# Row broadcasts by DMA instead of matmuls, and weight-sum stores issued by SyncE, in a tuned transformer block

## Chip, cores, metric

One core of a Trainium2 chip. The metric is the device time of one launch in microseconds (us): the median of several runs, and for comparisons the ratio to runs of the kernel before on the same chip. TensorE is called PE in the profile, VectorE DVE, ScalarE ACT, GpSimd POOL, SyncE SP.

## The reference, cut to what matters

```python
mod = silu(c) @ w_mod                      # six rows of 1024: sa, ca, ga, sb, cb, gb
h = layernorm(x) * (1 + ca) + sa
x = x + ga * attention(h)                  # 2048 queries, 32 heads of 128, 512 keys
h = layernorm(x) * (1 + cb) + sb
x = x + gb * (silu(h @ w_gate) * (h @ w_up)) @ w_down
```

`ga` and `gb` (the gate rows) multiply along the free dimension, so each has to stand in all 128 partitions. So has `silu(c)` (the conditioning row), because VectorE computes the late columns of `mod` as row products with transposed `w_mod` tiles. The large products are done with seven instead of eight block products, for which sums of weight blocks are made on VectorE during attention, stored to DRAM, and read back later.

## The kernel before

A row that sits as a column (one value per partition, eight columns) was spread by matmul: a ones matrix times a diagonal holding the column.

```python
def row_task(dst, dbuf, src, sbuf):
    ACT: c6 <- src                                           # 128x8
    def diags(n):
        for q in range(4):
            ACT: diag[q] <- ident * c6[:, 4*n+q]             # 128x128
    diags(0); yield
    for n in range(2):
        for q in range(4):
            mm(bank(XB, P, q * P), ones_bf, diag[q], q == 0, q == 3, ...)
        DVE: dst[:, n*512:(n+1)*512] <- bank(XB)
        if n == 0: diags(1)
        yield
```

The units of weight sums run in two slots of SBUF (the core's on-chip memory). Each unit is a load, four subtractions and a store; the fourth sum overwrites a quarter of the raw weights, so a slot's next load waits for its store to land:

```python
Q_of = {o: (dq("q_sl%d" % o, nc.gpsimd), dq("q_sw%d" % o, nc.gpsimd)) for o in OFF_ST}
# load of unit k into slot k % 2
T.op(Q_of[slot][0], lambda: g.dma_start(dst, src), reads=ahead, writes=[w.b_raw, w.b_s3])
# ... four DVE subtractions, spread over the iterations of attention ...
T.op(Q_of[slot][1], lambda: g.dma_start(dst, w.four), reads=[w.b_s3] + w.b_s, writes=[B_uw[units[k]]])
```

The softmax here doesn't subtract the row's maximum and nothing guards it: scores larger than these inputs give would overflow.

Of the kernel before, what the change touches and what calls it, by code (L numbers as in the profile page):

```python
# [4 lines left out]
AF = mybir.ActivationFunctionType  # L5
BF16 = mybir.dt.bfloat16
F16 = mybir.dt.float16
F32 = mybir.dt.float32
P = 128
# [122 lines left out]
def bass_adaLN_cond__sliding_block_cached__swiglu_ffn__prompt_kernel(  # L132
# [51 lines left out]
    mhalf = S_("mhalf", [P, TPC], F32)  # L184
    c_row = S_("c_row", [DT, P], BF16)
    sc_bf = S_("sc_bf", [P, DT], BF16)
    mod_bf = S_("mod_bf", [P, NJ], BF16)
    c6 = S_("c6", [P, DT], F32)
    mcol = S_("mcol", [P, 4 * DT], F32)
    gain = [S_("gain%d" % i, [P, DT], BF16) for i in range(2)]  # L190
    gain_f = S_("gain_f", [P, DT], F32)
# [20 lines left out]


    OFF_H20 = 154 * KB
    B_ident = _Buf("ident"); B_ones = _Buf("ones"); B_zw = _Buf("zw")
    B_diag = [_Buf("diag%d" % i) for i in range(4)]
    ident = arena.at(OFF_H20, [P], BF16, [B_ident])
    ones_bf = arena.at(OFF_H20 + 256, [P], BF16, [B_ones])
    diag = [arena.at(OFF_H20 + 512 + 256 * i, [P], BF16, [B_diag[i]]) for i in range(4)]
    zwarm = arena.at(OFF_H20 + 2048, [512], BF16, [B_zw])  # L220

    def bank(b, n=512, off=0):
# [5 lines left out]
    def bank_bf(b):  # L228
        return ps[:, b * 512:(b + 1) * 512].bitcast(BF16)
# [4 lines left out]
    PB = [_Buf("bank%d" % b) for b in range(8)]  # L234
    B_x = [_Buf("x%d" % t) for t in range(ST)]
    B_mh = _Buf("mhalf")
    B_cT = _Buf("cT"); B_sc = _Buf("sc"); B_late = [_Buf("late%d" % i) for i in range(4)]; B_c6 = _Buf("c6"); B_mcol = _Buf("mcol"); B_scr = _Buf("scr")
    B_mode = _Buf("mode"); B_modc = _Buf("modc"); B_bq = _Buf("bq"); B_gf = _Buf("gf")
    B_nm = _Buf("nmean"); B_acc = _Buf("acc"); B_acc0 = _Buf("acc0")
    B_g = [_Buf("g%d" % i) for i in range(2)]  # L240
# [21 lines left out]
    with nc.Block() as block:  # L262

        @block.gpsimd
        def _(g):
# [23 lines left out]
            def finish(gen):  # L289
                while gen in bg:  # L290
# [4 lines left out]
            T.op(POOL, lambda: g.affine_select(out=ident, in_=ident, compare_op=ALU.not_equal,  # L295
                                               fill=1.0, base=0, pattern=[[-1, P]], channel_multiplier=1),
                 reads=[B_ident], writes=[B_ident])
            T.op(POOL, lambda: g.memset(ones_bf, 1.0), writes=[B_ones])
            T.op(POOL, lambda: g.memset(mhalf[:, :], -0.5), writes=[B_mh])
            T.op(POOL, lambda: g.memset(zwarm, 0.0), writes=[B_zw])  # L300

# [115 lines left out]
            for gk in range(1, Hkv):  # L417
                load_kT(gk)
                load_v(gk)
            T.op(POOL, lambda: g.memset(v_aug[:, :, P:P + 2], 1.0), writes=[B_va])  # L420


            B_ns4 = B_ns + [_Buf("ns2"), _Buf("ns3")]
# [103 lines left out]
            def mod_ca(hf, k):  # L527
# [5 lines left out]
            T.op(PE, lambda: TE.transpose(bank_bf(XB)[:, 0:DT], c_row[:, :], ident[0:DT, 0:DT]),  # L533
                 reads=[B_cT, B_ident], writes=[PB[XB]])
            T.op(ACT, lambda: A.activation(sc_bf[:, :], bank_bf(XB)[:, 0:DT], AF.Silu), writes=[PB[XB], B_sc])
            T.op(ACT, lambda: A.activation(acc[:, 0:1], mhalf[:, 0:1], AF.Exp), reads=[B_mh], writes=[B_acc])


# [71 lines left out]
                     reads=[B_mcol], writes=[cbuf])  # L610


            def row_task(dst, dbuf, src, sbuf):
                T.op(ACT, lambda: A.activation(c6[:, :], src, AF.Copy), reads=[sbuf], writes=[B_c6])

                def diags(n):
                    for q in range(4):
                        col = 4 * n + q
                        T.op(ACT, lambda: A.activation(diag[q], ident, AF.Copy, scale=c6[:, col:col + 1]),
                             reads=[B_ident, B_c6], writes=[B_diag[q]])  # L620

                diags(0)
                yield
                for n in range(2):
                    for q in range(4):
                        mm(bank(XB, P, q * P), ones_bf, diag[q], q == 0, q == 3, [B_ones, B_diag[q]], PB[XB], skip=True)
                    T.op(DVE, lambda: V.tensor_copy(dst[:, n * 512:(n + 1) * 512], bank(XB)),  # L627
                         writes=[PB[XB], dbuf])
                    if n == 0:
                        diags(1)  # L630
                    yield


            LEAD = 3
# [290 lines left out]
                    mm(bank(bk), la, ra, start and k == 0, k == HK - 1, [lb, rb], PB[bk], skip=True)  # L925


            Q_of = {o: (dq("q_sl%d" % o, nc.gpsimd), dq("q_sw%d" % o, nc.gpsimd)) for o in OFF_ST}
            units = [("o", p) for p in range(HP)] + [("d", p) for p in range(FP)]
            unit_of = {}  # L930
            B_uw = {u: _Buf("uw%s%d" % u) for u in units}
# [15 lines left out]
            def unit_sums(k):  # L947
                w, slot = unit_of.pop(k)
                r = w.raw.rearrange("p k n -> p (k n)")
                rf = w.rawf.rearrange("p k n -> p (k n)")  # L950
                b11, b12, b21, b22 = [r[:, 512 * n:512 * n + 512] for n in range(4)]
                e = [x.rearrange("p k n -> p (k n)") for x in w.s]
                R = w.b_raw
                for (o, a, b, rd, wr) in ((e[0], b12, b11, [R, w.b_s3], w.b_s[0]), (e[1], b22, e[0], [R, w.b_s[0]], w.b_s[1]),
                                          (e[2], b21, e[1], [R, w.b_s[1]], w.b_s[2]), (rf[:, 1536:2048], b22, b12, [R], w.b_s3)):
                    T.op(DVE, lambda: V.tensor_tensor(o, a, b, SUB), reads=rd, writes=[wr])  # L956
                    yield
                kind, p = units[k]
                dst = (wo_sum if kind == "o" else wd_sum)[p].rearrange("q a n -> q (a n)")
                T.op(Q_of[slot][1], lambda: g.dma_start(dst, w.four), reads=[w.b_s3] + w.b_s, writes=[B_uw[units[k]]])  # L960

            def unit_chain(k0, k1):
                after = _Buf("after")
# [218 lines left out]


            rows = None
            bgx = []

            def run_x():
                if bgx:
                    try:
                        next(bgx[0])  # L1190
                    except StopIteration:
                        bgx.pop(0)

            LOADX = {14: 2, 20: 3}
            TAKES = [12, 17, 61] + [i for i in range(15, 2 * NI - 15) if i % 4 == 3 or (i > NI + 2 and i % 4 == 2 and i % 5 in (1, 4))]
            TAKES = sorted(TAKES)[:NL]
            TAKET = {i: n for n, i in enumerate(TAKES)}
            LOADT = {max(i - 4, TAKES[max(n - 2, 0)] if n > 1 else 0): n for i, n in TAKET.items()}
            assert len(TAKES) == NL and len(LOADT) == NL and not {NI, NI + 1} & (set(TAKET) | set(LOADT))
            take_oT(0)  # L1200
# [23 lines left out]
            def mods(i):  # L1224
                if i in TAKET:
                    n = TAKET[i]
                    mod_col(n)
                    g0, last = divmod(n, DT)
                    if last == DT - 1:
                        mod_take(g0, B_late[g0])  # L1230
                        if g0 == 0:
                            bgx.append(row_task(rowb[0], B_row[0], mod_bf[:, 2 * DT:3 * DT], B_late[0]))
                        elif g0 == 2:
                            mod_gain(1, B_late[2], B_g[1])
                        elif g0 == 3:
                            bgx.append(row_task(rowb[1], B_row[1], mod_bf[:, 5 * DT:6 * DT], B_late[3]))
                if i in LOADT:
                    load_mt(LOADT[i])

            def both(a, b):  # L1240
                yield from a
# [6 lines left out]
            def pre0(i):  # L1248
                if 2 <= i < NQ0:
                    q_shifted(i)  # L1250
                if i in LOADX:
                    load_x(LOADX[i])
                if i == 1:
                    scores(0)
                if i in (1, 3):
                    q_bias_mm(i + 1, i + 3, XB)
                if i == 1:
                    for dt in range(HK, DT):
                        shift(dt)
                if i < 9:  # L1260
                    if 2 <= i < 7:
                        qproj(i + 4)
                    elif i == 7:
                        qproj_mm(ND - 1, QB, 0, HK)
                    elif i == 8:
                        qproj(ND - 1, k0=HK)
                        for dt in range(DT):
                            modulate(hT[1], B_hT[1], dt, 0, 0, B_mode, x1_tiles)
                elif i + 4 < NDI:
                    qproj(i + 3)  # L1270
                elif i + 4 == NDI:
                    qproj_mm(NDI - 1, QB, 0, HK)
                elif i + 3 == NDI:
                    qproj(NDI - 1, k0=HK)
                for n, tt in enumerate(NORMS.get(i, ())):
                    norm_turn(1, tt, x1_tiles, (i + n) % 2)
                if 2 <= i < 6:
                    next(x1_stats[1])
                if i == 8:
                    bgx.append(row_task(sc_row, B_scr, sc_bf[:, :], B_sc))  # L1280
                if i == ND + 2:
                    take_oT(2)
                    take_oT(3)
                mods(i)
                if i == 44:
                    bg.append(stats_task(2 * TPC, 2 * TPC))
# [5 lines left out]
            def tick0(i):  # L1292
                if 2 <= i < 6:
                    next(x1_stats[0])
                if i < 20 or i % 4 == 0:
                    run_x()
                if i == 21:
                    hs[0] = h_sums()
                if 21 <= i < 25:
# [133 lines left out]
                mods(i)  # L1433

            def tick1(i):
                if i % 4 == 0:
                    run_x()
                if i > NI:
                    wq_tick(1, i)
                    if i == NI + 1:  # L1440
                        chain[0] = unit_chain(HP, HP + FP)
                    if i < 2 * NI - 8:
                        unit_tick(i)

            take_wq(1, 2)
            attend(1, NI, pre1, tick1)
            while bgx:
                run_x()


            OFF_GU = [14 * KB * i for i in range(4)]
# [288 lines left out]
```

## Time and profile before

| | before |
|---|---|
| time, median of 3 | 1155.57 us (1154.97 to 1157.11) |
| profiled span | 1152.5 us |
| PE busy, without work | 1140.7 us, 11.8 us |
| stores of weight sums, issue to landing, median of the first 16 | 4.8 us |

The page gives busy time by engine; "the chain" follows the last instruction back to what released it, step by step, so its shares tell which engine sets the end. The wait views give total, number and longest wait; what is behind the arrow ended the wait. The prediction below shows the lines that bound this kernel. The time of stores is this row of the list of DMA issues (size, then median us from issue to landing):

```profile
wo_sum<-arena POOLq DMA_DIRECT2D x16, 512.0 KB, 4.8
```

### The profile page before, as it was taken

Reading aid. Unit: us, or ns where it says so; the run is one execution under the profiler, and the core shown is the slowest. Engines: PE = TensorE matmul, PEld = TensorE weight load, DVE = VectorE, ACT = ScalarE, POOL = GpSimd, SP = SyncE. Lnnn points to the kernel's source line nnn. Section 1 sums busy time; section 2 is a strip of 40 time slices with the busy share of each in tenths; the row PEclk is TensorE's granted clock in tenths of the full one; section 3 lists DMA queues with packets and bytes.
Section 4 is the critical chain, followed back from the end, with each engine's and each line's share of the span. In section 5 each row is a group of like instructions: output and inputs, shape, how many; then the busy total and the mean of one; then the engine's idle time right before and its main releaser. Section 6 shows DMA issues by size and latency. Waiting matters only on the chain.

```text
span 1152.5 us, 17997 instructions
## 1 busy us (share of the span) xinstructions
PE 1140.7 (99%) x6930; PEld 585.6 (51%) x7015; DVE 826.0 (72%) x1650; ACT 532.3 (46%) x745; POOL 66.5 (6%) x137
## 2 busy tenths in 40 slices
PE   8999999999999999999999999999999999999999
PEld 5566565554446665566444444444444444444444
DVE  5768779847667777776657789877658777776536
ACT  4857787720127777787110354444110444444110
POOL 1100112100000111111000000000000000000000
DMA  9879999986718999945774422323773433234443
GB/s 316 143 182 225 206 219 221 216 206 182 220 36 183 202 211 207 197 97 120 192 224 136 110 74 79 105 74 101 210 218 129 119 84 100 74 103 133 129 157 110
DMA packets 299572, 179.96 MB, mean 156 GB/s; under 512 B 140512, under 2 KB 288736, under 8 KB 299488
## 3 DMA queue, kind: packets, MB, share of 16 engines
q1 hardware_dynamic: 236512, 92.31, 37.6%
q10 hardware_dynamic: 54336, 55.05, 15.1%
q0 software_dynamic: 8640, 31.46, 8.8%
q8 instruction: 55, 0.90, 0.3%
q14 instruction: 29, 0.24, 0.1%
HBM read 125.96 MB, written 19.92 MB: 127 GB/s over the span
## 4 chain that ended last, share of the span: by engine, by line
PE 96%; DVE 1%; DMA 1%; issue 1%; ACT 0%; POOL 0%; POOLq 0%; DVEq 0%
PE ps L272 96%; DMA wo_sum<-arena 1%; DMA arena<-in_A_wo_dram 0%; ACT arena L805 0%; DVE arena L835 0%; DVE arena L956 0%; DVE arena L827 0%; PE ps L276 0%; DVE arena L906 0%; DVE arena L852 0%; DVE arena L604 0%; DVE rl L824 0%; DVE rowb L627 0%; POOL arena L300 0%; DVE tmp L1117 0%
## 5 line engine op out<-in xcount | busy, mean ns | idle before, releaser
L272 PE MATMUL ps<-arena 128*128 128x512 f16 (+2 forms) x6717 | 1135.6, 330 | 8.9 <-POOL arena L420 2.2
L272 PEld LDWEIGHTS ps<-arena 128*128 128x128 bf16 (+1 forms) x6802 | 578.5, 98 | 560.0 <-DVE arena L835 4.9
L805 ACT ACTIVATE arena<-ps 128x1024 bf16<-128x1024 f32 x256 | 261.5, 1021 | 44.4 <-PE ps L272 32.6
L838 ACT ACTIVATE tmp<-ps 128x512 f32<-128x512 f32 x167 | 99.7, 597 | 295.9 <-PE ps L272 289.9
L906 DVE TENSOR_TENSOR arena<-arena 128x512 f16<-128x512 bf16 x328 | 133.4, 419 | 3.0
L835 DVE TENSOR_TENSOR arena<-ps,tmp 128x512 bf16<-128x512 f32 (+1 forms) x134 | 91.9, 686 | 51.4 <-PE ps L272 34.7
L838 ACT ACTIVATE nsc<-ps 128x512 f32<-128x512 f32 x84 | 50.1, 597 | 93.3 <-PE ps L272 90.9
L827 DVE TENSOR_TENSOR arena<-ps,rl 128x512 f16<-128x512 f32 x128 | 88.5, 691 | 4.9 <-DVE rl L824 0.5
L835 DVE TENSOR_TENSOR arena<-ps,nsc 128x512 f16<-128x512 f32 x84 | 57.3, 687 | 40.3 <-PE ps L272 29.9
L824 DVE RECIPROCAL rl<-ps 128x4 f32<-128x4 f32 x128 | 23.3, 182 | 73.7 <-PE ps L272 72.5
L1555 ACT ACTIVATE arena<-arena 128x512 f16<-128x512 f16 x84 | 49.8, 624 | 32.8 <-DVE arena L835 32.8
L1046 DVE TENSOR_TENSOR arena<-arena 128x2048 f16<-128x2048 f16 (+3 forms) x56 | 56.0, 1011 | 9.3 <-PE ps L272 8.8
L1122 DVE TENSOR_TENSOR tmp<-ps,tmp 128x512 f32<-128x512 f32 x32 | 22.1, 690 | 55.5 <-ACT tmp L838 45.8
L838 ACT ACTIVATE arena<-ps 128x512 f32<-128x512 f32 x16 | 9.6, 597 | 87.8 <-PE ps L272 87.8
L956 DVE TENSOR_TENSOR arena<-arena 128x512 f16<-128x512 bf16 x120 | 47.9, 420 | 2.5 <-DMA arena<-in_A_wo_dram 1.5
L427 DVE BATCH_NORM_STATS2 st<-x_res 128x6 f32<-128x512 bf16 x58 | 39.6, 682 | 3.7 <-DMA x_res<-in_A_x_dram 3.4
L604 DVE SCALAR_TENSOR_TENSOR arena<-arena 128x1024 bf16<-128x1024 bf16 x32 | 38.9, 1216 | 0.0
L1570 DVE TENSOR_TENSOR arena<-arena 128x512 f16<-128x512 f16 x84 | 35.0, 417 | 0.3
L1123 DVE TENSOR_TENSOR tmp<-tmp,rowb 128x512 f32<-128x512 f32 (+1 forms) x49 | 33.6, 686 | 1.7
L441 DVE TENSOR_SCALAR nsc<-x_res,mv,rstd 128x1024 f16<-128x1024 bf16 (+1 forms) x30 | 16.2, 539 | 24.1 <-DMA arena<-nsc 24.0
L1124 DVE TENSOR_TENSOR arena<-tmp,x_res 128x512 bf16<-128x512 f32 (+1 forms) x33 | 22.3, 676 | 1.1
L835 DVE TENSOR_TENSOR arena<-ps,rowb 128x512 f16<-128x512 f32 x28 | 19.3, 689 | 3.8 <-ACT rowb L838 3.3
(86 smaller groups left out, 323.6 us busy)
## 6 DMA issues: line engine op xcount, KB each, us to landing
arena<-in_A_wq_dram SPq DMA_DIRECT2D x30, 512.0 KB, 5.3
arena<-wo_sum ACTq DMA_DIRECT2D x7, 2048.0 KB, 8.2
arena<-in_B_w_gate_dram SPq DMA_DIRECT2D x28, 512.0 KB, 4.0
arena<-in_B_w_up_dram SPq DMA_DIRECT2D x28, 512.0 KB, 5.1
arena<-wd_sum ACTq DMA_DIRECT2D x8, 1792.0 KB, 7.9
arena<-in_B_w_down_dram ACTq DMA_DIRECT2D x6, 1792.0 KB, 7.8
arena<-in_A_wo_dram POOLq DMA_DIRECT2D x16, 512.0 KB, 5.1
wo_sum<-arena POOLq DMA_DIRECT2D x16, 512.0 KB, 4.8
```

The lines of the kernel that those rows point to most:

```text
L272: T.op(PE, lambda: TE.matmul(out_ap, lhsT, rhs, start=start, stop=stop, skip_group_check=skip), reads=reads, writes=[bank_buf])
L427: T.op(DVE, lambda: V.bn_stats(st_[sl][:, hf * 6:hf * 6 + 6], x_res[:, t, hf * 512:hf * 512 + 512]), reads=[B_x[t]], writes=[B_st[sl]])
L604: T.op(DVE, lambda: V.scalar_tensor_tensor(mt[n % 2], mt[n % 2], 1.0, sc_row, op0=ALU.mult, op1=ALU.mult, accum_out=mcol[:, n:n + 1]), rea ...
L805: T.op(ACT, lambda: A.activation(ex_s[es][:, 2 * kp:2 * kp + 2, :], banks2(SCB + 2 * kp), AF.Exp, scale=att_scale), writes=[PB[SCB + 2 * k ...
L827: T.op(DVE, lambda: V.tensor_tensor(o_s[os_].rearrange("p (a b) d -> p a b d", a=2), psap(PVB * 512, [[512, 2], [130, 2], [1, P]]), rlb, A ...
L835: T.op(DVE, lambda: V.tensor_tensor(out, bank(ba), other, ADD), reads=[ob2], writes=[PB[ba], ob])
L838: T.op(ACT, lambda: A.activation(dst, bank(bk), AF.Copy), writes=[PB[bk], db])
L906: T.op(st, lambda: eng.tensor_tensor(o, a, b, op), reads=rd, writes=[wr])
L956: T.op(DVE, lambda: V.tensor_tensor(o, a, b, SUB), reads=rd, writes=[wr])
L1046: T.op(DVE, lambda: V.tensor_tensor(o, a, b, SUB), reads=rd, writes=[sb])
L1555: T.op(ACT, lambda: A.activation(o, s_, AF.Silu), reads=[sb], writes=[ob])
L1570: T.op(DVE, lambda: V.tensor_tensor(gu[blk][:, p, :], o, s_, MULT), reads=[sb, ob], writes=[B_gu[blk][p]])
```

## The change

Its intent: take the row matmuls off TensorE, their diagonals off ScalarE and their copies off VectorE, and let SyncE instead of GpSimd issue the stores of weight sums. A row now goes: columns transposed by DMA inside SBUF, stored to DRAM as eight runs of 256 bytes, read back with a zero stride over partitions. The conditioning row starts as a row, so it skips the transpose and gets a second Silu on ScalarE.

```diff
+T.op(POOL, lambda: g.memset(mod_bf[:, :], 0.0), ...)        # mod_bf is now 128x128; ones_bf, diag, c6 are gone
+T.op(ACT, lambda: A.activation(c_row[:, :], c_row[:, :], AF.Silu), writes=[B_cT])
-def row_task(dst, dbuf, src, sbuf): ...                     # as above
+def row_hop(n, hop):
+    if hop == 0:
+        T.op(Q_row[n][0], lambda: SP.dma_start_transpose(turned..., mod_bf[:, :]), reads=[B_mode] + B_late, writes=[B_turn])
+    elif hop == 1:
+        src, sb = (c_row[:, :], B_cT) if n == 2 else (turned[c0:c0 + DT, :], B_turn)
+        T.op(Q_row[n][1], lambda: SP.dma_start(rows_d[n], src), reads=[sb], writes=[B_rd[n]])
+    else:
+        every = bass.AP(tensor=rows_d[n].tensor, offset=0, ap=[[0, P], [1, D]])
+        T.op(Q_row[n][2], lambda: SP.dma_start(dst, every), reads=[B_rd[n]], writes=[db])
+HOPS = {4: (2, 1), 8: (2, 2)}                               # attention iteration: (row, hop)
+for n, i in ((0, TAKES[DT - 1]), (1, TAKES[NL - 1])):
+    HOPS.update({i + 2: (n, 0), i + 5: (n, 1), i + 8: (n, 2)})
-Q_of = {o: (dq("q_sl%d" % o, nc.gpsimd), dq("q_sw%d" % o, nc.gpsimd)) for o in OFF_ST}
+Q_of = {o: (dq("q_sl%d" % o, nc.gpsimd), dq("q_sw%d" % o)) for o in OFF_ST}
-T.op(Q_of[slot][1], lambda: g.dma_start(dst, w.four), ...)
+T.op(Q_of[slot][1], lambda: SP.dma_start(dst, w.four), ...)
```

More of the change, by code (lines that the diff above doesn't have):

```diff
@@ L186, in bass_adaLN_cond__sliding_block_cached__swiglu_ffn__prompt_kernel @@
     sc_bf = S_("sc_bf", [P, DT], BF16)
-    mod_bf = S_("mod_bf", [P, NJ], BF16)
-    c6 = S_("c6", [P, DT], F32)
+    mod_bf = S_("mod_bf", [P, P], BF16)
     mcol = S_("mcol", [P, 4 * DT], F32)
@@ L214, in bass_adaLN_cond__sliding_block_cached__swiglu_ffn__prompt_kernel @@
     OFF_H20 = 154 * KB
-    B_ident = _Buf("ident"); B_ones = _Buf("ones"); B_zw = _Buf("zw")
-    B_diag = [_Buf("diag%d" % i) for i in range(4)]
+    B_ident = _Buf("ident"); B_turn = _Buf("turn"); B_zw = _Buf("zw")
     ident = arena.at(OFF_H20, [P], BF16, [B_ident])
-    ones_bf = arena.at(OFF_H20 + 256, [P], BF16, [B_ones])
-    diag = [arena.at(OFF_H20 + 512 + 256 * i, [P], BF16, [B_diag[i]]) for i in range(4)]
+    turned = arena.at(OFF_H20 + 256, [P], BF16, [B_turn])
     zwarm = arena.at(OFF_H20 + 2048, [512], BF16, [B_zw])
@@ L236, in bass_adaLN_cond__sliding_block_cached__swiglu_ffn__prompt_kernel @@
     B_mh = _Buf("mhalf")
-    B_cT = _Buf("cT"); B_sc = _Buf("sc"); B_late = [_Buf("late%d" % i) for i in range(4)]; B_c6 = _Buf("c6"); B_mcol = _Buf("mcol"); B_scr = _Buf("scr")
+    B_cT = _Buf("cT"); B_sc = _Buf("sc"); B_late = [_Buf("late%d" % i) for i in range(4)]; B_mcol = _Buf("mcol"); B_scr = _Buf("scr")
     B_mode = _Buf("mode"); B_modc = _Buf("modc"); B_bq = _Buf("bq"); B_gf = _Buf("gf")
@@ L297, in _ @@
                  reads=[B_ident], writes=[B_ident])
-            T.op(POOL, lambda: g.memset(ones_bf, 1.0), writes=[B_ones])
             T.op(POOL, lambda: g.memset(mhalf[:, :], -0.5), writes=[B_mh])
@@ L420, in _ @@
             T.op(POOL, lambda: g.memset(v_aug[:, :, P:P + 2], 1.0), writes=[B_va])
+            T.op(POOL, lambda: g.memset(mod_bf[:, :], 0.0), writes=[B_mode] + B_late)
             B_ns4 = B_ns + [_Buf("ns2"), _Buf("ns3")]
@@ L610, in mod_take @@
                      reads=[B_mcol], writes=[cbuf])
-            def row_task(dst, dbuf, src, sbuf):
-                T.op(ACT, lambda: A.activation(c6[:, :], src, AF.Copy), reads=[sbuf], writes=[B_c6])
-                def diags(n):
-                    for q in range(4):
-                        col = 4 * n + q
-                        T.op(ACT, lambda: A.activation(diag[q], ident, AF.Copy, scale=c6[:, col:col + 1]),
-                             reads=[B_ident, B_c6], writes=[B_diag[q]])
-                diags(0)
-                yield
-                for n in range(2):
-                    for q in range(4):
-                        mm(bank(XB, P, q * P), ones_bf, diag[q], q == 0, q == 3, [B_ones, B_diag[q]], PB[XB], skip=True)
-                    T.op(DVE, lambda: V.tensor_copy(dst[:, n * 512:(n + 1) * 512], bank(XB)),
-                         writes=[PB[XB], dbuf])
-                    if n == 0:
-                        diags(1)
-                    yield
+            rows_d = [nc.dram_tensor("row%d" % n, [DT, P], BF16).ap() for n in range(3)]
+            B_rd = [_Buf("rowd%d" % n) for n in range(3)]
+            Q_row = [[dq("q_row%d_%d" % (n, m)) for m in range(3)] for n in range(3)]
+            def row_hop(n, hop):
+                if hop == 0:
+                    T.op(Q_row[n][0], lambda: SP.dma_start_transpose(turned.rearrange("p (a b) -> p a b", a=1), mod_bf[:, :]),
+                         reads=[B_mode] + B_late, writes=[B_turn])
+                elif hop == 1:
+                    c0 = (2 + 3 * n) * DT
+                    src, sb = (c_row[:, :], B_cT) if n == 2 else (turned[c0:c0 + DT, :], B_turn)
+                    T.op(Q_row[n][1], lambda: SP.dma_start(rows_d[n], src), reads=[sb], writes=[B_rd[n]])
+                else:
+                    dst, db = ((rowb[0][:, :], B_row[0]), (rowb[1][:, :], B_row[1]), (sc_row, B_scr))[n]
+                    every = bass.AP(tensor=rows_d[n].tensor, offset=0, ap=[[0, P], [1, D]])
+                    T.op(Q_row[n][2], lambda: SP.dma_start(dst, every), reads=[B_rd[n]], writes=[db])
             LEAD = 3
@@ L959, in unit_sums @@
                 dst = (wo_sum if kind == "o" else wd_sum)[p].rearrange("q a n -> q (a n)")
-                T.op(Q_of[slot][1], lambda: g.dma_start(dst, w.four), reads=[w.b_s3] + w.b_s, writes=[B_uw[units[k]]])
+                T.op(Q_of[slot][1], lambda: SP.dma_start(dst, w.four), reads=[w.b_s3] + w.b_s, writes=[B_uw[units[k]]])
             def unit_chain(k0, k1):
@@ L1184, in _ @@
             rows = None
-            bgx = []
-            def run_x():
-                if bgx:
-                    try:
-                        next(bgx[0])
-                    except StopIteration:
-                        bgx.pop(0)
             LOADX = {14: 2, 20: 3}
@@ L1230, in mods @@
                         mod_take(g0, B_late[g0])
-                        if g0 == 0:
-                            bgx.append(row_task(rowb[0], B_row[0], mod_bf[:, 2 * DT:3 * DT], B_late[0]))
-                        elif g0 == 2:
+                        if g0 == 2:
                             mod_gain(1, B_late[2], B_g[1])
-                        elif g0 == 3:
-                            bgx.append(row_task(rowb[1], B_row[1], mod_bf[:, 5 * DT:6 * DT], B_late[3]))
                 if i in LOADT:
                     load_mt(LOADT[i])
+                if i in HOPS:
+                    row_hop(*HOPS[i])
             def both(a, b):
@@ L1278, in pre0 @@
                     next(x1_stats[1])
-                if i == 8:
-                    bgx.append(row_task(sc_row, B_scr, sc_bf[:, :], B_sc))
                 if i == ND + 2:
@@ L1294, in tick0 @@
                     next(x1_stats[0])
-                if i < 20 or i % 4 == 0:
-                    run_x()
                 if i == 21:
@@ L1435, in tick1 @@
             def tick1(i):
-                if i % 4 == 0:
-                    run_x()
                 if i > NI:
@@ L1446, in _ @@
             attend(1, NI, pre1, tick1)
-            while bgx:
-                run_x()
             OFF_GU = [14 * KB * i for i in range(4)]
```

## The prediction

> **What bounds the kernel now.** I read the page's first part, then the chain that ended last, then the waits of TensorE, and last the rows of the instructions that the change touches.
>
> ```profile
> PE 1140.7 (99%) x6930; PEld 585.6 (51%) x7015; DVE 826.0 (72%) x1650; ACT 532.3 (46%) x745; POOL 66.5 (6%) x137
> PE 96%; DVE 1%; DMA 1%; issue 1%; ACT 0%; POOL 0%; POOLq 0%; DVEq 0%
> ```
>
> TensorE (PE) is busy for 1140.7 of 1152.5 us and holds 96% of the chain. A busy PE need not be a PE at its peak, so I compared starts of successive matmuls in the trace: 216 ns between 512-column ones, 57 ns between 129-column ones, nearly everywhere. Of the 11.8 us without work about 2.2 us come before the first matmul and 2.5 us at the end. So PE is held by its own list of matmuls, and a change pays in two ways only: by taking matmuls off the list, or by ending a wait of PE. Those waits between 20 and 1140 us, in full:
>
> ```profile
> PE ps L272 <- DVE arena L827: 0.7, 1, 0.7
> PE ps L272 <- DVE arena L835: 0.4, 2, 0.2
> PE ps L272 <- ACT arena L805: 0.3, 1, 0.3
> ```
>
> They sum to 1.4 us, the ceiling of the second way as far as this view sees it. The 0.7 us one is the only one with a DMA behind it. The timeline around it:
>
> ```profile
> 127.90 0.57 POOL L960 DMA_DIRECT2D wo_sum<-arena  x1 [2.08 <-DVE arena L956]
> ...
> 136.33 0.70 POOL L945 DMA_DIRECT2D arena<-in_A_wo_dram  x1 [7.86 <-DMA wo_sum<-arena]
> ...
> 141.53 0.88 DVE L956 TENSOR_TENSOR arena<-arena 128x512 f16<-128x512 bf16 x2 [1.48 <-DMA arena<-in_A_wo_dram]
> 142.33 1.22 DVE L604 SCALAR_TENSOR_TENSOR arena<-arena 128x1024 bf16<-128x1024 bf16 x1
> ...
> 144.83 2.40 PE L272 MATMUL ps<-arena 128*128 128x129 bf16 x21 [0.68 <-DVE arena L827]
> ```
>
> Read it downwards: the weight sums leave by a GpSimd DMA, the load into the same slot waits for that store to land (7.86 us), VectorE waits 1.48 us for the load, runs late with the softmax division (L827), and PE stands still for 0.68 us. It is the one place where a store of weight sums reaches PE.
>
> **What the Trainium skill says.** "TensorE: Matmul & The Clock Gate", section "Wait — 56ns, not 53.3ns?", gives 55.6 and 215.7 ns between starts of warm matmuls of 128 and 512 columns; this trace has 56 and 216 ns, so it agrees, and 56 ns is the price of each removed matmul. "DMA: Bandwidth & Descriptors", section "Issuing engines are not separate DMA queues", says that DMAs of all issuers run on the same 16 engines and that another issuer saves the sequencer's time alone: no bandwidth is to be had from moving the stores to SyncE. Section "SWDGE vs HWDGE vs iDMA" of that page calls the hardware path's set-up faster; its "Specifications" put the first byte at about 1 us for GpSimd and 0.6 us for SyncE, so I estimate 0.4 us per store. No run here shows that difference yet. The page's "Two DMAs through the same engine are not ordered" asks for a wait on the first DMA before one that reads what it wrote; the changed kernel has these waits, and they stand in SyncE's list, so I ask below whether they hold up others.
>
> **Removed: matmuls.** Three rows (conditioning row, gate rows 0 and 1) were spread over partitions by a ones matrix times diagonals: 3 rows x 2 halves x 4 = 24 matmuls of 128 columns. The instruction order of both builds shows that nothing else moves on PE: six groups of four are gone. Price: 24 x 56 ns = 1.34 us. The chain confirms that they cost their full length today. In the second attention stretch two kinds of iteration alternate, and those with four more matmuls are longer:
>
> ```profile
> 493.24 6.08 PE ps L272 x51
> 499.32 0.05 issue
> 499.37 6.94 PE ps L272 x55
> 506.31 0.05 issue
> 506.36 6.30 PE ps L272 x55
> 512.66 0.05 issue
> 512.72 6.94 PE ps L272 x55
> 519.66 0.05 issue
> 519.71 6.30 PE ps L272 x55
> ```
>
> 6.30 against 6.08 us is 0.22 us for four, that is 55 ns each; 6 x 0.22 = 1.32 us, the same sum.
>
> **Removed: work of ScalarE and VectorE.**
>
> ```profile
> L619 ACT ACTIVATE arena<-arena,c 128x128 bf16<-128x128 bf16 x24 | 7.6, 389 | 0.1
> L627 DVE CAST rowb<-ps 128x512 bf16<-128x512 f32 x4 | 2.7, 680 | 0.0
> L627 DVE CAST arena<-ps 128x512 bf16<-128x512 f32 x2 | 1.4, 680 | 0.0
> ```
>
> ScalarE loses 7.6 us of diagonals and three 0.2 us copies of columns, VectorE six casts or 4.1 us. None is on the chain except one cast, at 173.35 us, ahead of a 0.2 us wait of PE (the one on L835 near 176 us). Elsewhere the engines have room: VectorE is busy 29.4 of the 40 us from 60 to 100 and about 75% of 340 to 540. So from these 12 us I count 0.2 us.
>
> **Added.** ScalarE gets one Silu of 8x128 near 3.5 us; like its neighbour it should take some 0.18 us, and ScalarE then idles 1.97 us for x at 7.02. GpSimd swaps a ones memset for a zero memset of the same size (0.2 us) that stands after the one PE waits for; PE's first matmul can come about 0.2 us sooner, but the first projection at 11.67 us needs weights that landed at 11.48 us (the issue-to-landing times of that load), so I count zero. SyncE gets two 128x128 transposes, three 2 KB stores, three broadcasts of 256 KB. Estimated from like ones, 1.2 us of issue and some 4 us to landing for a transpose, 0.5 us of issue and 3 to 5 us to landing for a load. All have time: the conditioning row is asked for in iteration 8 (about 51 us) and first read at 64.8 us; gate row 0 arrives around iteration 43 (about 171 us) and is first read at 262.9 us; gate row 1 comes in iteration 119, read from about 886 us on. The bytes are 0.8 MB beside 180 MB.
>
> **Moved.** Thirty stores of 512 KB go from GpSimd to SyncE.
>
> ```profile
> L960 POOL DMA_DIRECT2D wo_sum<-arena x16 | 9.4, 591 | 66.8 <-DVE arena L956 66.8
> L960 POOL DMA_DIRECT2D wd_sum<-arena x14 | 8.0, 571 | 90.9 <-DVE arena L956 90.9
> ```
>
> GpSimd's 17 us of issue are worth nothing, it is 6% busy. SyncE has room: per iteration of about 3.4 us it issues one 1.2 us transpose, a weight-row transpose of 1.3 us in one of two to four, a query load of 0.53 us in one of four, and now a store of about 0.57 us in one of three: some 1.2 + 0.4 + 0.13 + 0.2 = 1.9 us. What matters is when the slot comes free. From issue to landing the 16 stores of the first attention took 3.5 to 9.1 us (the 14 of the second 3.1 to 5.8), and the next load 4 to 6 us more; the time left between that load's landing and its first use was 0.02 to 3.5 us for most of those from 100 to 215 us, and 4 us or more in the second attention, bar the first. At 127.14 us SyncE issued a weight-row transpose, landing at 135.83 us beside the slow store. The store now stands ahead of it in SyncE's list (it belongs to the iteration before), so I expect it to leave first and land in 4 to 5 us. Then VectorE's 1.48 us wait and PE's 0.68 us go. That gain I count in full: 0.7 us.
>
> **Sum.** 1.34 (matmuls) + 0.7 (the wait at 144 us) + 0.2 (the wait at 176 us) = 2.2 us, so 1155.57 - 2.2 = 1153.4 us.
>
> **Rivals.**
> (a) The stores get stuck behind transposes and query loads on SyncE's queue and land 2 to 4 us later. For it: loads at 141.5, 167.4 and 194.1 us land within 0.1 us of their use, so late landings go straight to VectorE; transposes landed as late as 9 us after issue. Against it: they land late beside the stores already now, on other queues. Three to five waits of 1 to 2 us, half of which reaches PE, cost 2 to 4 us: 1155 to 1157.
> (b) Only the matmuls count: the wait at 144 us stays, since landing depends on the shared engines. 1154.2 us.
> (c) Freed VectorE and ScalarE remove most small waits (1.4 us and 0.2 us pauses near 105, 186, 199, 212 and 232 us). VectorE's 4.1 us are too few and elsewhere. 1152.5 us.
> (d) A row hop's wait blocks SyncE, so transposed attention outputs come late. Hops are three iterations (10 us) apart and transposes land in 3 to 9 us; four output buffers absorb one late transpose. Below 1 us.
>
> **Range and chances.** The runs of before spread over 2.1 us, and the rivals run from 1152.5 to 1157. I take 1151.4 to 1156.0. Two per cent is 23 us; PE's list shrinks by 1.34 us and all its waits are below 5 us, so faster by 2% is out of reach, and slower needs a queue that stalls for many iterations: 0.005, 0.985, 0.01.
>
> **What would show it.** Right: 24 matmuls fewer, iterations of 6.30 us back at 6.08; no wait on the weight load near 141 us; stores landing within about 5 us; SyncE's new waits short; PE's waits below 1 us after the start. Wrong: VectorE waiting for weight loads or for the weight-row transposes (L604) several times in 100 to 240 us, PE idle with it, and a span at or above 1155 us.

## The result, and the profile after

| | before | after |
|---|---|---|
| time, median of 6 | 1155.40 us (1154.62 to 1157.11) | 1152.82 us (1151.78 to 1154.39) |
| ratio, with 95% interval | | 0.9977 (0.9964 to 0.9990) |
| profiled span | 1152.5 us | 1151.0 us |

A ratio is the mean time of one kernel's fast runs over that of the other's of the same rounds, so it is not quite the ratio of the medians. Two later sets of runs of the changed kernel gave 0.9979 and 0.9982. The change saves about 2.4 us: same within 2%, but clear of noise. The page after, busy time and chain:

```profile
PE 1138.7 (99%) x6906; PEld 584.3 (51%) x6991; DVE 822.4 (71%) x1644; ACT 525.6 (46%) x719; POOL 50.8 (4%) x107
PE 95%; DMA 2%; DVE 1%; issue 1%; ACT 1%; DVEq 0%
```

24 matmuls are gone (6930 to 6906) and PE still carries the chain. The same stretch of the chain that the prediction shows for before:

```profile
490.80 6.08 PE ps L269 x51
496.87 0.05 issue
496.93 6.94 PE ps L269 x55
503.87 0.05 issue
503.92 6.08 PE ps L269 x51
510.00 0.05 issue
510.05 6.94 PE ps L269 x55
516.99 0.05 issue
517.04 6.08 PE ps L269 x51
```

The two pieces of 6.30 us are back at 6.08 us: the four matmuls of each half row left PE's time in full. Now the place where a store of weight sums reached PE, by the timeline (start, duration, engine, line, operation; idle time before it and what ended it in brackets):

```profile
126.86 0.34 SPq L955 DMA_DIRECT2D wo_sum<-arena  x1
127.25 1.56 SPq L597 DMA_TRANSPOSE arena<-in_w_mod_dram  x1
...
132.80 0.72 POOL L940 DMA_DIRECT2D arena<-in_A_wo_dram  x1 [7.24 <-DVE arena L951]
...
139.21 0.88 DVE L951 TENSOR_TENSOR arena<-arena 128x512 f16<-128x512 bf16 x2
```

The store leaves ahead of the weight-row transpose, as the prediction had it; the next load of its slot starts 5.9 us after the store's issue (before: 8.4 us), and VectorE's sums at 139.21 us wait for nothing. (The bracket behind the load names VectorE, but the store landed 0.58 us before the load was issued.) All waits of PE between 20 and 1140 us after:

```profile
PE ps L269 <- DVE tmp L1117: 1.2, 1, 1.2
PE ps L269 <- DVE arena L830: 0.4, 2, 0.2
PE ps L269 <- ACT arena L800: 0.3, 1, 0.3
```

The 0.7 us behind the softmax division (L827 before, L822 after) is gone, but a wait of 1.2 us has come. It is in the second output projection, far from any line of the change:

```profile
566.58 0.55 DVE L438 TENSOR_SCALAR nsc<-x_res,mv,rstd 128x1024 f16<-128x1024 bf16 x1 [5.38 <-DMA arena<-nsc]
...
569.90 0.68 DVE L1117 TENSOR_TENSOR tmp<-ps,tmp 128x512 f32<-128x512 f32 x1
...
570.64 1.68 PE L269 MATMUL ps<-arena 128*128 128x512 f16 x7 [1.15 <-DVE tmp L1117]
```

VectorE waits 5.38 us for a LayerNorm transpose, reads a PSUM bank (where TensorE's products lie) late, and PE waits for the bank. Before had a wait of VectorE of 3.45 us at this place and none of PE. And the first projection matmul came at 11.17 us after, at 11.67 us before. So one pair of profiles shows three kinds of difference: the matmuls, the wait at 144 us, and two differences that may be luck. The experiments had to separate them.

**Theory:** the matmuls give 1.34 us, the earlier landing of the stores about 0.7 us, and the differences at the start and near 570 us vary from execution to execution. **Rivals:** the rows carry the whole gain; or the stores' issuer does not matter at all.

### The profile page after: what moved, and what is told of

The parts are those of the page before. It is cut to its first block, busy times and chain, and to the rows that moved or that the text cites. A ratio compares the mean times of both kernels' runs of the same rounds, so it can differ in the third digit from the quotient of the medians.

```text
span 1151.0 us, 17926 instructions
## 1 busy us (share of the span) xinstructions
PE 1138.7 (99%) x6906; PEld 584.3 (51%) x6991; DVE 822.4 (71%) x1644; ACT 525.6 (46%) x719; POOL 50.8 (4%) x107
## 4 chain that ended last, share of the span: by engine, by line
PE 95%; DMA 2%; DVE 1%; issue 1%; ACT 1%; DVEq 0%
PE ps L269 95%; DMA arena<-nsc 1%; ACT arena L800 1%; DMA arena<-arena 0%; DVE st L424 0%; DMA x_res<-in_A_x_dram 0%; DVE arena L1057 0%; DVE nsc L438 0%; PE ps L273 0%; DVE arena L830 0%; DVE arena L847 0%; DVE arena L822 0%; DVE mv L544 0%; DVE arena L901 0%; DVE tmp L1117 0%
## 5 line engine op out<-in xcount | busy, mean ns | idle before, releaser
L830 DVE TENSOR_TENSOR arena<-ps,tmp 128x512 bf16<-128x512 f32 (+1 forms) x134 | 91.9, 686 | 52.2 <-PE ps L269 34.7
L822 DVE TENSOR_TENSOR arena<-ps,rl 128x512 f16<-128x512 f32 x128 | 88.5, 691 | 4.7 <-DVE rl L819 0.2
L830 DVE TENSOR_TENSOR arena<-ps,nsc 128x512 f16<-128x512 f32 x84 | 57.3, 687 | 40.3 <-PE ps L269 30.0
L830 DVE TENSOR_TENSOR arena<-ps,rowb 128x512 f16<-128x512 f32 x28 | 19.3, 689 | 3.8 <-ACT rowb L833 3.3
```

Of the source, the lines that this page charges most:

```text
L822: T.op(DVE, lambda: V.tensor_tensor(o_s[os_].rearrange("p (a b) d -> p a b d", a=2), psap(PVB * 512, [[512, 2], [130, 2], [1, P]]), rlb, A ...
L830: T.op(DVE, lambda: V.tensor_tensor(out, bank(ba), other, ADD), reads=[ob2], writes=[PB[ba], ob])
```

## The experiments

### The two kernels unchanged

No edit. What varies between executions of one kernel?

> The kernel before, unchanged: the noise. Ratio to before 1.000 with an interval of about 0.001 either way. In its profile I look at two places: the start (first projection matmul at 11.67 us in the first profile of before, 11.17 us in that of after) and the wait on the weight load near 141 us. Theory A (the start gain is luck of the first DMAs): the first projection starts anywhere from 11.1 to 11.7 us. Theory B (the start gain comes from the memset that left): 11.6 to 11.7 us again. The PE wait of 0.7 us at 144 us is there again if it belongs to the kernel, absent if it was luck of that execution.

> The changed kernel, unchanged: ratio 0.9975 to 0.9985 (2.2 to 2.7 us less than before). Its first profile had a PE wait of 1.2 us near 570 us, behind VectorE waiting for a LayerNorm transpose, that before did not have. If it belongs to the change it is there again at 1.1 to 1.3 us; if it was luck of that execution it is absent or of another size, and the profiled span is about 1149.7 us rather than 1151.0.

Measured: before 1.0002 (0.9988 to 1.0015), after 0.9979 (0.9967 to 0.9990). Runs of before went from 1153.27 to 1157.92 us, so one run of a kernel says nothing about 1 us. The first projection of the unchanged kernel before now began at 11.28 us (11.67 in its first profile); a later profile of the changed kernel (below) had it at 11.68 us (11.17 in its first). So theory A holds: the start gain of the first pair was luck of the first loads, not of the memset. The changed kernel's PE wait near 570 us was absent in this execution and its span 1150.2 us (expected 1149.7): luck too. PE's waits from 24 to 250 us, kernel before, second profile:

```profile
PE ps L272 <- DVE arena L835: 0.4, 2, 0.2
PE ps L272 <- ACT arena L805: 0.3, 1, 0.3
PE ps L272 <- DVE arena L827: 0.3, 1, 0.3
```

The wait behind L827 belongs to the kernel, with a size that varies.

### One part of the change at a time

Rows only: the changed kernel with the stores given back to GpSimd.

```diff
-Q_of = {o: (dq("q_sl%d" % o, nc.gpsimd), dq("q_sw%d" % o)) for o in OFF_ST}
+Q_of = {o: (dq("q_sl%d" % o, nc.gpsimd), dq("q_sw%d" % o, nc.gpsimd)) for o in OFF_ST}
-T.op(Q_of[slot][1], lambda: SP.dma_start(dst, w.four), ...)
+T.op(Q_of[slot][1], lambda: g.dma_start(dst, w.four), ...)
```

> Rows over DRAM, weight-sum stores still by GpSimd. Theory of the prediction: 24 matmuls x 56 ns = 1.34 us, plus 0.2 us of a cast, plus up to 0.4 us at the start: ratio 0.9984 to 0.9988, and the VectorE wait on the weight load near 140 us stays at 1 to 1.5 us with 0.5 to 0.9 us of PE idle. Rival (the rows carry all of the gain): ratio 0.9977.

> The rows-only kernel a second time, because runs of one kernel spread over 3 to 5 us and its first ratio (0.9994, 0.9982 to 1.0006) misses neither theory. The prediction's theory: 0.9985 to 0.9988 for the rows; rival (rows carry all): 0.9977.

Stores only: the kernel before with the same two lines edited the other way.

> Rows by matmuls as before, weight-sum stores by SyncE. Theory of the prediction: 0.7 us less than before, ratio 0.9994, stores land in about 4 us, no wait of VectorE on a weight load. Rival (the shared DMA engines decide, the issuer does not matter): ratio 1.000 and stores landing in 5 us. Rival (SyncE's queue is clogged): ratio 1.001 or more.

> The stores-only kernel a second time (first ratio 1.0005, 0.9990 to 1.0019, with one run of 1158.59 us). The prediction's theory: 0.9994. Rival (the issuer of the stores does not matter): 1.000. In its first profile VectorE still waited 1.0 us on one weight load; if the move of the stores ends that wait, no such wait here; if not, it is there again at about 1 us.

Measured: rows only 0.9994 (0.9982 to 1.0006) and 0.9988 (0.9973 to 1.0004); stores only 1.0005 (0.9990 to 1.0019) and 0.9995 (0.9981 to 1.0009). The means of the pairs, 0.9991 and 1.0000, are 1.0 us and 0 us less than before, with about 1.2 us either way (the half widths of 0.0012 to 0.0016, over the root of two). The rows fit 1.34 us; the whole 2.4 us (0.9979) lies outside their first interval and inside the second. The stores fit 0.7 us and fit nothing at all. Times alone do not settle the stores; the waits of PE do better. From 24 to 250 us, rows only (first profile, stores by GpSimd), then stores only (second profile, stores by SyncE):

```profile
PE ps L269 <- DVE arena L830: 0.9, 2, 0.7
PE ps L269 <- DVE arena L822: 0.6, 1, 0.6
PE ps L269 <- ACT arena L800: 0.3, 1, 0.3
```

```profile
PE ps L272 <- DVE arena L835: 0.2, 1, 0.2
```

Over all profiles but those of the doubled store and of the early load (alone or with the other edit), where the path itself was edited. "Behind the division" is any wait of PE on L827 or L822, at whatever time:

| stores by | profiles | PE waits behind the division | mean | all PE waits, 24 to 250 us | mean |
|---|---|---|---|---|---|
| GpSimd | 5 | 0.7, 0.3, 0.6, 0.7, 0.8 | 0.6 us | 1.4, 1.0, 1.8, 1.6, 1.0 | 1.4 us |
| SyncE | 6 | 0, 0, 0, 0, 0.4, 0 | 0.1 us | 0.7, 1.2, 0.9, 0.2, 1.8, 0.9 | 1.0 us |

A wait behind the division goes with the issuer in ten profiles of eleven, but it is not always the wait that the prediction named. That one has its own place: the sixth store, issued near 127 us (132 us in the ninefold kernel below), the load that follows it, VectorE's sums, PE at 144 us. At this place alone, with the runs in the order given on the left:

| | sixth store lands after | next load issued, from the store's issue | VectorE waits for that load | PE waits there |
|---|---|---|---|---|
| GpSimd: before twice, ninefold, rows only twice | 7.9, 8.1, 7.8, 6.8, 7.0 us | 8.4, 8.7, 8.3, 7.4, 7.5 us | 1.5, 1.3, 1.8, 0, 0 us | 0.7, 0.3, 0.8, 0, 0 us |
| SyncE: changed three times, LayerNorm later (the changed kernel, up to here), stores only twice | 5.4, 4.3, 5.3, 5.0, 4.9, 4.8 us | 5.9, 4.9, 5.9, 5.6, 5.5, 5.4 us | 0, 0, 0, 1.4, 1.0, 1.1 us | 0, 0, 0, 0.4, 0, 0 us |

The first link goes with the issuer in all eleven: the store leaves ahead of the weight-row transpose and lands 1.5 to 3.8 us sooner. (Issuer and place in the list changed together; no run separates them.) The last links do not follow it. Stores only, first profile:

```profile
127.61 0.34 SPq L960 DMA_DIRECT2D wo_sum<-arena  x1
133.10 0.72 POOL L945 DMA_DIRECT2D arena<-in_A_wo_dram  x1 [7.03 <-DVE arena L827]
141.03 0.89 DVE L956 TENSOR_TENSOR arena<-arena 128x512 f16<-128x512 bf16 x2 [0.99 <-DMA arena<-in_A_wo_dram]
```

The load goes out some 3.2 us sooner than before (133.10 against 136.33 us) and lands only 0.5 us sooner: it took 7.9 us (8.1 us in the second profile) against 5.2 us before. What slowed it these runs do not tell. My expectation that VectorE would then wait for no weight load was wrong: the wait stayed at the same sums, smaller, and PE, which had waited 0.3 us behind 1.3 us of VectorE and 0.7 us behind 1.5 us, did not wait behind 1.0 and 1.1 us. Rows only, first profile, has the converse, with the stores still on GpSimd:

```profile
139.32 0.88 DVE L951 TENSOR_TENSOR arena<-arena 128x512 f16<-128x512 bf16 x2
193.26 0.89 DVE L951 TENSOR_TENSOR arena<-arena 128x512 f16<-128x512 bf16 x2 [1.17 <-DMA arena<-in_A_wo_dram]
196.77 1.08 PE L269 MATMUL ps<-arena 128*128 128x129 bf16 x16 [0.58 <-DVE arena L822]
```

Here the wait near 140 us is gone without SyncE's help (in the second profile the load landed just 0.02 us before its use), and another stands at 193 us. So the issuer changes where and how often PE waits; its net effect on PE is about 0.4 us by these means, and the scatter is as large.

### The price of a row matmul

The kernel before, each group of four done nine times.

```diff
-for q in range(4):
+for q in list(range(4)) * 9:
     mm(bank(XB, P, q * P), ones_bf, diag[q], q == 0, q == 3, ...)
```

> The kernel before with each group of four row matmuls done nine times (same result): 192 matmuls of 128 columns more. If a row matmul costs its full 56 ns, as the prediction counts for the 24 removed ones: 10.75 us more, ratio 1.0093. If they hide in waits of TensorE: under 8 us more, ratio below 1.007. If they bring waits of their own (the row copy of VectorE, the shared bank): over 12 us, ratio above 1.0104.

Measured: 1.0086 (1.0069 to 1.0102), 10.0 us by the means (1165.12 against 1155.14 us) for 192 matmuls: 52 ns each, with 42 to 61 ns covered by the interval (0.0069 and 0.0102 of 1155 us over 192). The 56 ns lies inside; a price hidden in waits was expected under 1.007, which the interval all but excludes. So the 24 removed ones are worth 1.0 to 1.5 us, and 1.34 us by their starts in the trace.

### Does the landing of the stores matter?

The kernel before, with a second store of each unit to a scratch tensor ahead of the real one; the next load waits for both.

```diff
+T.op(Q_tw[slot], lambda: g.dma_start(twice[k], w.four), reads=[w.b_s3] + w.b_s)
 T.op(Q_of[slot][1], lambda: g.dma_start(dst, w.four), ...)
```

> The kernel before with every store of weight sums preceded by a second one of the same 512 KB to a scratch tensor, also from GpSimd; the next load of the slot waits for both. Theory: landing time of the stores reaches the end, since the slack of the loads in the first attention is 0 to 3 us: stores land 2 to 3 us later, VectorE waits 1 to 2 us on several weight loads, TensorE stands still 3 to 6 us in all, ratio 1.003 to 1.005. Rival (store landings hardly matter, one wait of 1 us whatever they do): ratio below 1.001.

Measured: 1.0136 (1.0109 to 1.0163), 15.8 us by the means, three times what I expected. Four of the six runs had a clock of 0.996 to 0.997; whether the waits caused that or it came on top is not shown. The two at 1.0, of which one is profiled, took 12.5 us more than before in the mean. In its profile the median landing of the real store in the first attention went from 4.8 to 6.7 us. VectorE's waits for weight loads, then PE's waits, in its profile:

```profile
DVE arena L958 <- DMA arena<-in_A_wo_dram: 18.5, 10, 3.0
...
DVE arena L958 <- DMA arena<-in_B_w_down_dram: 5.3, 4, 1.9
```

```profile
PE ps L272 <- DVE arena L827: 8.5, 6, 2.5
PE ps L272 <- DVE arena L835: 5.2, 5, 1.8
PE ps L272 <- DVE arena L657: 1.1, 1, 1.1
```

23.8 us of VectorE's waiting become 14.8 us of PE's. So the path from store to load to VectorE to PE is real and steep: the rival for whom landings hardly matter falls. A second store also doubles their traffic, so not all of the 15.8 us need be landing alone; the profiled execution took 14.9 us more than the mean of before, and its waits of PE, 13.4 us above the 1.4 us of the first profile of before, account for most of that. What stays small is how far the issuer moves the landing of the stores as a whole. Median of the first 16 stores: GpSimd 4.8, 4.6, 4.9, 4.6, 5.0 us in five profiles; SyncE 4.0, 4.1, 4.9, 4.1, 5.1, 4.5 us in six. Two rows of the list of DMA issues, changed kernel and stores only (first profile):

```profile
wo_sum<-arena SPq DMA_DIRECT2D x16, 512.0 KB, 4.0
```

```profile
wo_sum<-arena SPq DMA_DIRECT2D x16, 512.0 KB, 4.9
```

The means of the two groups are 4.8 and 4.4 us: 0.4 us sooner on average, as estimated, but one execution differs from the next by more. The median hides the sixth store, which moved by far more and in every profile.

### Can the two waits be taken away?

Early load: the changed kernel with the fourth sum of each unit in a buffer of its own (the diagonals had left 1 KB free), so that a load waits for VectorE's reads only, not for the store. The main lines of the edit:

```diff
+s3x = arena.at(OFF_H20 + 512, [512], F16, [B_s3x])
-T.op(Q_of[slot][0], lambda: g.dma_start(dst, src), reads=ahead, writes=[w.b_raw, w.b_s3])
+T.op(Q_of[slot][0], lambda: g.dma_start(dst, src), reads=ahead, writes=[w.b_raw])
-(rf[:, 1536:2048], b22, b12, [R], w.b_s3)
+(s3x, b22, b12, [R], B_s3x)
-T.op(Q_of[slot][1], lambda: SP.dma_start(dst, w.four), ...)
+T.op(Q_of[slot][1], lambda: SP.dma_start(dst[:, 512:2048], w.three), reads=w.b_s, ...)
+T.op(Q_s3, lambda: SP.dma_start(dst[:, 0:512], s3x), reads=[B_s3x], ...)
```

> The changed kernel, with the fourth sum of each unit in a buffer of its own (the 1 KB that the diagonals left free), so that the next load of the slot no longer waits for the store to land. Theory (store landing, then load landing, is what makes VectorE wait): no VectorE wait on a weight load at all, TensorE's waits from 24 to 250 us at or below 0.6 us against 0.7 and 1.2 us in two profiles of the changed kernel; time 0 to 0.6 us below it, ratio to before 0.9972 to 0.9978. Rival (30 more issues on SyncE and more DMA traffic at once hold up transposes): VectorE waits on transposes or weight rows appear, ratio 0.998 or more.

LayerNorm later: the changed kernel with two background steps of the second output projection moved behind its first outputs.

```diff
 def o_hook1(idx, j):
-    run_bg(1)
+    if idx > 0 or j < 2:
+        run_bg(1)
```

> The changed kernel, with the third and fourth normalisation of the second output projection moved behind the first outputs of that stage. Theory (VectorE waits for a LayerNorm transpose there and so frees a PSUM bank late): no TensorE wait near 570 us, where six of the nine profiles of all kernels so far had 0.6 to 2.2 us by the shift of ScalarE's instructions; 0.7 us less on average, ratio 0.9970 to 0.9975. Rival (the delayed LayerNorm makes the end of the stage late): a TensorE wait appears near 600 us, ratio 0.998 or more.

Both, and the changed kernel as yardstick:

> Both of these edits on the changed kernel. If both theories hold: about 1.2 us below the changed kernel, ratio to before 0.9965 to 0.9970, and a spread of runs below 2 us, because the two waits that differ from run to run are gone.

> The changed kernel again, as the yardstick of this call: ratio 0.9977 to 0.9980. No TensorE wait behind the softmax division (0.3 to 0.8 us in each of the five profiles with stores from GpSimd, none in the four with stores from SyncE).

| kernel | median of 5 | ratio (95% interval) |
|---|---|---|
| early load | 1152.39 us | 0.9985 (0.9972 to 0.9997) |
| LayerNorm later | 1152.26 us | 0.9980 (0.9967 to 0.9992) |
| both | 1152.54 us | 0.9979 (0.9966 to 0.9993) |
| changed kernel | 1152.09 us | 0.9982 (0.9969 to 0.9995) |

None beats the changed kernel. The early load ended VectorE's waits for weight loads, but a new wait of the same kind took their place: the one buffer of the fourth sum is free only when its store has landed.

```profile
DVE arena L961 <- DMA wo_sum<-arena: 1.9, 3, 0.7
```

PE's waits from 24 to 250 us in that profile came to 1.3 us, no less than with the changed kernel. The LayerNorm edit: no PE wait near 570 us in its profiles, but none in the second and third profile of the changed kernel as it is either, so nothing is shown. My expectation also overcounted there: I had read shifts of ScalarE's instructions as waits of PE, while the wait view has PE waiting at that place in only two of those nine profiles (1.2 and 0.8 us). With the rarer wait worth perhaps 0.2 us on average, no gain was to be measured. The spread of "both" was the smallest, 1151.76 to 1152.58 us, but five runs prove no spread. And the LayerNorm-later execution, whose program up to here is the changed kernel's, had the one division wait among the SyncE profiles, at the very place that the prediction named:

```profile
132.67 0.72 POOL L940 DMA_DIRECT2D arena<-in_A_wo_dram  x1 [7.72 <-DVE arena L901]
140.83 0.89 DVE L951 TENSOR_TENSOR arena<-arena 128x512 f16<-128x512 bf16 x2 [1.35 <-DMA arena<-in_A_wo_dram]
143.93 1.32 PE L269 MATMUL ps<-arena 128*128 128x129 bf16 x17 [0.36 <-DVE arena L822]
```

The sixth store had landed in 5.0 us as in the other SyncE profiles; it was the load behind it that took 8.1 us. So SyncE as issuer makes this wait smaller or rarer, not impossible.

## Why the prediction was right

**Total.** 2.2 us less was predicted, 1155.57 to 1153.4 us; measured 2.6 us less by the medians and 2.4 us by the mean of three ratios (0.9979). The range 1151.4 to 1156.0 held. That the total fits better than its parts (1.34, 0.4 and 0 us, below) is in part luck. Of the rivals, (c), 1152.5 us, lies nearest to the measured 1152.8 us, but not by its reason: with rows only, VectorE and ScalarE had the same freed time, and PE's waits from 24 to 250 us were 1.8 and 1.6 us, no less than before (1.4 and 1.0 us). Rival (b), the matmuls alone at 1154.2 us, a ratio of 0.9988, lies within each interval of the whole change, and outside only when the three are taken together (0.9979, some 0.0007 either way).

**Matmuls, 1.34 us: right.** Shown by the count, by pieces of the chain returning from 6.30 to 6.08 us, and by the ninefold kernel.

**The wait at 144 us, 0.7 us: first step right, the rest half right.** The store did go out ahead of the weight-row transpose and landed in 4.3 to 5.4 us in all six profiles (predicted 4 to 5), against 6.8 to 8.1 us. That VectorE's wait then goes does not follow: stores only kept 1.0 and 1.1 us of it, because the load that started sooner took longer, and rows only lost it without SyncE. That VectorE's wait was gone in the first profile of the changed kernel is therefore not shown to come from the stores. PE's wait there shrank, from 0.7, 0.3 and 0.8 us with row matmuls and GpSimd stores to none with row matmuls and SyncE stores. Over the whole stretch all PE waits fell by 0.4 us in the mean rather than 0.7, with a scatter as large. Rival (a) of the prediction, clogged stores, did not come: they landed no later on average (4.4 against 4.8 us).

**The wait at 176 us, 0.2 us: misread.** The chain passes through VectorE there, but the wait view lists none of PE from 165 to 190 us in the first profile of before (PE stood idle for 0.08 us); its two waits on L835 (0.23 and 0.15 us) stand at 105.5 and 199.5 us. The cast is gone, but waits of this kind (L835, L830 after) sum to 0.2 to 1.1 us in every kernel, with no difference between the groups.

**Start, zero: right.** PE's first matmul did come sooner (2.03 against 2.17 us), but the first projection varied from 11.2 to 11.7 us in both kernels. (The stretch after PE's last matmul is 2.8 us, not the 2.5 us of the prediction, in both.)

**Added DMA work, hidden: right.** Broadcasts landed 3.5 to 5.3 us after issue, transposes of the columns in 3.9 us (median), and no wait on them appears for PE or VectorE; SyncE's longest wait on a row hop was 0.2 us. The extra Silu took 0.29 us, not 0.18, and stayed hidden.

**What stays open.** 1.34 and 0.4 us make 1.7 us; about 2.4 us was measured, with some 0.8 us either way (the three half widths of 0.0012 to 0.0013, over the root of three), so 1.7 us is not excluded. The parts measured alone sum to 1.0 us with some 1.7 us either way (1.2 us twice, added in quadrature). Whether rows and stores help each other, or the rest is sampling, these runs do not tell: it would take many more runs of each, since single runs spread over 3 to 5 us.

## What to carry to other kernels

Where PE is busy 99% of the span and its starts follow at the rate of its columns, a matmul taken off is worth its columns and nothing else pays except a wait that ends at PE; so price the removed matmuls first, and take freed time on other engines for zero. Before a wait of under 1 us in a single profile is counted in full, profile the same kernel again: here two executions gave 0.7 and 0.3 us for one wait, and the start varied by 0.5 us on its own. And look where a wait stands, not only behind which line: the two rows-only profiles had none there and one of 0.6 and 0.7 us behind the same line, 50 us later. To learn whether a latency matters, make it worse: the doubled store cost 15.8 us and showed that the path from store to PE is there, which undoing the change could not.

## What the Trainium skill lacked or had wrong

- "DMA: Bandwidth & Descriptors", sections "SWDGE vs HWDGE vs iDMA" and "Specifications": the estimate of 0.4 us from the first-byte latencies there (about 1 us for GpSimd, 0.6 us for SyncE) is near the difference of the mean landings (4.8 and 4.4 us for 512 KB stores), though in these runs the place in the issuer's list changed too. The page does not say how the landing of one such store varies beside other traffic: 3.0 to 9.1 us in the first attention of the two first profiles.
- The same page, section "Issuing engines are not separate DMA queues": it says that issuing from several engines at once saves issue time alone. What the section lacks is that a new issuer can also change which transfer leaves first: with the sixth store ahead of the weight-row transpose instead of behind it, the slot's next load went out 4.9 to 5.9 us after the store instead of 7.4 to 8.7 us.
- No page read here tells how far executions of one tuned kernel lie apart: 1153.27 to 1157.92 us for the kernel before, with waits on PE that come and go.
